# One transfer issued as two: the first weight load of a decode kernel in pieces of 16 and 112 partitions

## The chip, the cores and the metric

The kernel runs on one core of one Trainium2 chip. The metric is device time in microseconds (us): the median of three runs, 722.08 us before the change, the runs lying between 721.86 and 722.98 us. A core has five engines that this text names as the profile does: PE (TensorE, matrix products), DVE (VectorE), ACT (ScalarE), POOL (GpSimd) and SP (SyncE, which here only issues transfers). Sixteen DMA engines move data between the memory (HBM) and the on-chip tiles, which have 128 partitions.

## The reference

One decode step for two sequences, all in float32: attention over a cache of 4096 positions with 32 heads of 128, beside a small dense network, mixed by a gate.

```python
g = sigmoid((x * gate_w).sum(-1, keepdims=True))          # x: (2, 1, 576)
q = (x @ wq).reshape(B, 1, 32, 128).transpose(0, 2, 1, 3)   # wq: (576, 4096)
p = softmax(einsum("bhqd,bhkd->bhqk", q, k_cache) * 128 ** -0.5)
o = einsum("bhqk,bhkd->bhqd", p, v_cache)                    # caches: (2, 32, 4096, 128)
a = o.transpose(0, 2, 1, 3).reshape(B, 1, 4096) @ wo         # wo: (4096, 576)
b = gelu(x @ w1 + b1) @ w2 + b2                              # w1: (576, 4608)
return g * a + (1 - g) * b
```

The two caches are 134 MB each, the four weight matrices together some 40 MB. Every byte is used once.

## The kernel before, in words

**Ring.** One tile, `ring`, holds three slots of 128 partitions x 16384 floats (64 KB a partition, 8.4 MB a slot). Everything that comes from HBM in bulk lands there. The order of the transfers is written out by hand in `seq`: wq in two loads (`("wq", 0)` and `("wq", 1)`), w1 in three, then for each of sixteen units `i` a tile of the key cache and a tile of the value cache (`load_heads`, line 130), then three batches with w2 and wo (`load_last`, line 145). `load()` takes the next entry; every bulk transfer is issued by SP on one queue, in this order.

**The first transfer.** `load_w(wq, (4,), 0)` takes the first 512 rows of wq, four rows to a partition. Each partition gets 4 x 4096 floats in one piece, 65,536 bytes, and the transfer fills slot 0 as a whole: 128 partitions, 8.4 MB. It is the first instruction of SP's queue (line 119). The remaining 64 rows of wq follow as 128 partitions x 8 KB, then w1 as two loads of 128 x 36 KB and one of 128 x 9 KB, all from line 119.

**The small inputs.** ACT issues four kinds of small transfers on a queue of its own: `load_b1(0)` (line 195, four rows of 4.6 KB to partitions 0, 32, 64 and 96), two rows of x (line 200) and the gate weights (line 201). They are issued in the first microseconds, beside the first bulk transfer, and later `load_b1(1)` and b2 (line 294).

**Start of the computation.** PE turns x and the gate weights into columns (line 249), forms the gate sum (line 258), and then `proj` multiplies x with wq (line 282 into `qps`) as soon as all of the first load is there. From q, q's rows are spread over the partitions (`q_unit`), and `proj` does the same with w1 (line 282 into `hps`). Each of these steps frees a slot, and SP waits for that before it issues the next cache tile.

**Units.** For each unit DVE multiplies the key tile by q (`mul`, line 457), DVE and POOL reduce it (`red`, lines 461 to 463), DVE takes a maximum (`max_p`, line 467), ACT forms the exponentials (line 482), and PE multiplies them with the value tile (`av`, line 493). A new tile is issued when the one three places earlier in the ring has been used up (`load_next`).

**End.** The last three batches bring w2 and wo in ever smaller pieces; the last product is in line 415, the output leaves by line 438, two rows of 2.3 KB.

**Counters.** Each transfer counts its completion on one of eight counters for transfers issued by SP and ACT, taken in turn; a transfer that takes a counter again waits until the transfer that had it before has landed. Such waits stand on the issuing engine (SP or ACT), ahead of the transfer.

Of the kernel before, what the change touches and what calls it, by code (L numbers as in the profile page):

```python
# [12 lines left out]
P = 128  # L13
# [6 lines left out]
def kernel(  # L20
# [14 lines left out]
    nc = tc.nc  # L35
# [69 lines left out]
    used = {"w": 0, "t": (WQ + F) * D // P}  # L105
# [3 lines left out]
    def load_w(w, rows, c):  # L109
        if c < len(rows):  # L110
            n = rows[c] * w.shape[1]
            lo = sum(rows[:c]) * P
            src = w[lo:lo + rows[c] * P].rearrange("(p r) n -> p (r n)", r=rows[c])
        else:
            n = w.shape[1] // 2
            src = w[NX * P:].rearrange("q (e n) -> (q e) n", e=2)
        t = ring[:, used["w"]:used["w"] + n]
        used["w"] += n
        nc.sync.dma_start(t, src)
        return t  # L120

    def slot(n):
# [27 lines left out]
    def temp(n, parts=P):  # L150
        t = ring[:parts, used["t"]:used["t"] + n]
        used["t"] += n
        assert used["t"] <= SLOTS * SLOT
        return t
# [7 lines left out]
    def load():  # L162
        if not seq:
            return
        kind, i = seq.pop()
        if kind == "wq":
            wqt[i] = load_w(wq, ROWS[kind], i)
        elif kind == "w1":
            w1t[i] = load_w(w1, ROWS[kind], i)
        elif kind == "k":  # L170
            kt[i] = load_heads(k_cache, i)
        elif kind == "v":
            vt[i] = load_heads(v_cache, i)
        else:
            load_last(i)
        if kind in ("k", "v", "last"):
            held.append((kind, i))
# [41 lines left out]
    for j in range(NPB):  # L219
        t = cp.tile([P, NT * EB + 32 - EB], F32, name=f"p{j}")  # L220
# [156 lines left out]
    t = temp(NF * B).rearrange("p (r b) -> p r b", b=B)  # L377
# [223 lines left out]
```

## Time and profile before

| what | value |
|---|---|
| median of 3 runs | 722.08 us (721.86 to 722.98) |
| the profiled execution, first to last instruction (its span) | 720.1 us |
| mean granted TensorE clock in the span | 0.666 |
| bytes read from HBM | 308.59 MB, 429 GB/s over the span |
| busy share: PE, DVE, ACT, POOL | 33%, 72%, 5%, 20% |
| SP's queue of bulk transfers: share of the 16 DMA engines' time | 99.2% |

For the profiled execution only the span is given, and no device time of its own; the median of the unprofiled runs lies 2.0 us above the span. A group of lines in the profile reads: line, engine, operation, tile written <- tile read, count, busy time, mean duration, and the idle time ahead of it with what ended it. "SPq" and "ACTq" are the issuing sides of SP and ACT; a line with DMA_DIRECT2D is the issue of a transfer, not the transfer itself. The DMA lines give the mean busy share of the 16 DMA engines by slice of the window, in tenths.

### The profile page before, as it was taken

How to read it: one execution, taken by the hardware profiler on the slowest of the kernel's cores; microseconds unless marked ns; L12 is line 12 of the kernel's file. 1: busy time of each engine (PE TensorE's matmuls, PEld its weight loads, DVE VectorE, ACT ScalarE, POOL GpSimd, SP SyncE). 2: the span in 40 equal slices, each digit the busy share in tenths (PEclk: the TensorE clock that was granted, in tenths of full speed). 3: DMA queues.
4: the chain of work that ended last, by engine and by line, in shares of the span. 5: the costliest groups of instructions: out<-in, count | busy, mean ns of one | idle time of the engine just before them, and what ended most of it. 6: DMA issues, size and time to landing. Idle time of an engine off the chain costs nothing.

```text
span 720.1 us, 3893 instructions
## 1 busy us (share of the span) xinstructions
PE 237.1 (33%) x1661; PEld 72.7 (10%) x1661; DVE 517.7 (72%) x150; ACT 37.8 (5%) x141; POOL 143.2 (20%) x28
## 2 busy tenths in 40 slices
PE   0755022140516060604142140506060503324197
PEld 0321000010101010101010000101010101001033
DVE  0004969879696969696969879696969596978900
ACT  0010010100101010101010100101010101010000
POOL 1000130404050403022040404040503113040400
PEclk9967557575757575665757575757575665757589
DMA  9999999999999999999999999999999999999997
GB/s 409 411 443 430 433 440 415 459 416 451 422 444 420 437 433 426 442 430 440 434 433 440 426 434 433 430 433 434 440 430 444 423 448 422 444 426 430 422 427 299
DMA packets 7101, 308.84 MB, mean 429 GB/s; under 512 B 798, under 2 KB 1182, under 8 KB 1580
## 3 DMA queue, kind: packets, MB, share of 16 engines
q1 hardware_dynamic: 7060, 308.55, 99.2%
q8 instruction: 13, 0.21, 0.1%
q10 hardware_dynamic: 24, 0.05, 0.0%
q14 instruction: 4, 0.03, 0.0%
HBM read 308.59 MB, written 0.00 MB: 429 GB/s over the span
## 4 chain that ended last, share of the span: by engine, by line
DMA 46%; DVE 35%; PE 17%; ACT 1%; issue 1%; POOL 0%; ACTq 0%; DVEq 0%; SPq 0%; POOLq 0%
DMA ring<-in_A_k_cache_dram 39%; DVE ring L457 19%; DVE s L462 10%; PE av L493 9%; DVE s L463 5%; DMA ring<-in_A_wo_dram 3%; DMA ring<-in_gate_w_dram 3%; PE qps L282 2%; PE hps L282 2%; PE oall L511 1%; PE acc L346 1%; PE mt L472 1%; ACT p L482 1%; DMA ring<-in_B_b_dram 1%; PE qps L307 1%
## 5 line engine op out<-in xcount | busy, mean ns | idle before, releaser
L457 DVE TENSOR_TENSOR ring<-ring,q 128x16384 f32<-128x16384 f32 x16 | 275.6, 17225 | 102.2 <-DMA ring<-in_A_k_cache_dram 102.2
L461 POOL TENSOR_TENSOR ring<-ring 128x3968 f32<-128x3968 f32 x16 | 137.1, 8566 | 487.4 <-DVE ring L457 457.3
L462 DVE TENSOR_REDUCE s<-ring 128x66 f32<-128x8448 f32 x16 | 143.3, 8953 | 1.3
L493 PE MATMUL av<-ring,p 128*32 128x512 f32 x1024 | 134.4, 684 | 11.4 <-ACT p L482 6.1
L472 PE MATMUL mt<-idsc,m 128*128 128x128 f32 x32 | 12.7, 501 | 365.9 <-DVE m L467 365.9
L463 DVE TENSOR_REDUCE s<-ring 128x62 f32<-128x3968 f32 x16 | 68.4, 4276 | 0.0
L482 ACT ACTIVATE p<-s,bs 32x128 f32<-32x128 f32 x64 | 25.5, 398 | 483.0 <-DVE bs L476 481.8
L493 PEld LDWEIGHTS av<-ring,p 128*32 128x32 f32 x1024 | 35.8, 125 | 119.6 <-issue 102.9
L472 PEld LDWEIGHTS mt<-idsc,m 128*128 128x128 f32 x32 | 8.0, 312 | 382.1 <-DVE m L467 353.5
L330 PE MATMUL qb<-qm,spread 64*128 64x512 f32 x8 | 8.3, 1137 | 69.8 <-POOL qm L326 69.8
L511 PE MATMUL oall<-avs,pick 128*64 128x512 f32 x32 | 30.6, 1059 | 0.8 <-DVE avs L505 0.8
L505 DVE TENSOR_TENSOR avs<-av,selr 128x512 f32<-128x512 f32 x16 | 10.9, 681 | 15.9 <-PE av L493 15.9
L369 DVE TENSOR_TENSOR ring<-hps,ring 128x384 f32<-128x384 f32 x3 | 1.7, 559 | 17.4 <-PE hps L282 17.3
L240 DVE COPY ring<-ring 3x64 f32<-3x64 f32 x2 | 0.3, 182 | 19.0 <-DMA ring<-in_gate_w_dram 19.0
L326 POOL TENSOR_TENSOR qm<-qall,mine 64x512 f32<-64x512 f32 x4 | 4.1, 1034 | 46.2 <-ACT qall L309 46.2
L301 DVE COPY ring<-ident 128x8 f32<-128x8 f32 x8 | 0.7, 169 | 16.9 <-DMA ring<-in_B_b_dram 16.9
L482 ACT ACTIVATION_READ_ACCUMULATOR p<-s,bs 32x1 f32 x64 | 11.8, 184 | 0.0
L282 PE MATMUL qps<-ring 128*32 128x512 f32 x80 | 11.6, 746 | 0.0
L282 PE MATMUL hps<-ring 128*32 128x384 f32 x120 | 11.5, 547 | 0.0
L346 PE MATMUL acc<-ring,hg 128*2 128x288 f32 x144 | 11.4, 453 | 0.0
L437 DVE COPY ring<-res 2x144 f32<-2x144 f32 x2 | 0.6, 300 | 12.7 <-PE res L415 12.7
L330 PEld LDWEIGHTS qb<-qm,spread 64*128 64x128 f32 x8 | 2.0, 307 | 72.9 <-POOL qm L326 72.9
(80 smaller groups left out, 75.2 us busy)
## 6 DMA issues: line engine op xcount, KB each, us to landing
ring<-in_B_w_dram SPq DMA_DIRECT2D x2, 4608.0 KB, 34.5
ring<-in_B_w_dram SPq DMA_DIRECT2D x2, 4032.0 KB
ring<-in_A_wo_dram SPq DMA_DIRECT2D x2, 2880.0 KB, 19.3
ring<-in_B_w_dram SPq DMA_DIRECT2D x1, 2304.0 KB, 13.3
ring<-in_A_wo_dram SPq DMA_DIRECT2D x2, 864.0 KB
ring<-in_B_w_dram SPq DMA_DIRECT2D x1, 1152.0 KB
ring<-in_A_wo_dram SPq DMA_DIRECT2D x1, 1152.0 KB
ring<-in_A_wq_dram SPq DMA_DIRECT2D x1, 1024.0 KB, 24.1
```

What stands on the lines that cost most here:

```text
L282: nc.tensor.matmul(ps[32 * j:32 * j + 32, :width], lhs, ts[c][:, o:o + width], start=(k == 0), stop=last, skip_group_check=True,)
L330: nc.tensor.matmul(ps, spread, t.rearrange("p u d -> p (u d)"), start=True, stop=True)
L346: nc.tensor.matmul(acc[o:o + m], lhsT, rhs[:, s * DS:(s + 1) * DS], start=start, stop=stop, skip_group_check=True)
L457: nc.vector.tensor_mul(kt[i], kt[i], qs[i].unsqueeze(1).to_broadcast([P, R, DH]))
L461: nc.gpsimd.tensor_add(t[:, :, :DH2], t[:, :, :DH2], t[:, :, DH2:])
L462: nc.vector.tensor_reduce(st[i][:, HALVED:], kt[i][:, HALVED:], AX.X, ALU.add)
L463: nc.vector.tensor_reduce(st[i][:, :HALVED], t[:, :, :DH2], AX.X, ALU.add)
L472: nc.tensor.matmul(mt[i], mx[i].to_broadcast([P, P]), idsc, start=True, stop=True)
L482: nc.scalar.activation(p[w, :, e * RB:(e + 1) * RB], st[i][w].rearrange("p (t c) -> p t c", c=RB), AF.Exp, bias=bias[i][w, e:e + 1], scale ...
L493: nc.tensor.matmul(ps[32 * j:32 * j + 32], p[:, EB * t:EB * t + 32], vt[i][:, RB * t:RB * (t + 1)].rearrange("p r d -> p (r d)"), start=(t ...
L505: nc.vector.tensor_mul(t, avs[i].rearrange("p (r d) -> p r d", d=DH), selr.unsqueeze(2).to_broadcast([P, RB, DH]))
L511: nc.tensor.matmul(oall, pick[:, NO - E - i * E:2 * NO - E - i * E], avs[i].rearrange("p r d -> p (r d)"), start=(i == 0), stop=(i == N - ...
```

## The change

In `load_w`, the transfer that fills the start of the ring is issued as two: partitions 0 to 15 (1.05 MB) first, then partitions 16 to 127 (7.34 MB). All other loads have `first = P` and are issued as before. The destination, the data and everything that reads them stay. SP's queue has one more transfer, and the transfers behind it take the next of the eight counters, so some of the waits on counters that SP and ACT make name another earlier transfer.

```diff
             src = w[NX * P:].rearrange("q (e n) -> (q e) n", e=2)
         t = ring[:, used["w"]:used["w"] + n]
+        first = 16 if used["w"] == 0 else P
         used["w"] += n
-        nc.sync.dma_start(t, src)
+        for a, z in ((0, first), (first, P)):
+            if a < z:
+                nc.sync.dma_start(t[a:z], src[a:z])
         return t
```

## The prediction

> **What bounds the kernel now.** I began with the page: the span, its slices, the queues.
>
> ```profile
> span 720.1 us, 3893 instructions
> PE 237.1 (33%) x1661; PEld 72.7 (10%) x1661; DVE 517.7 (72%) x150; ACT 37.8 (5%) x141; POOL 143.2 (20%) x28
> DMA  9999999999999999999999999999999999999997
> q1 hardware_dynamic: 7060, 308.55, 99.2%
> HBM read 308.59 MB, written 0.00 MB: 429 GB/s over the span
> ```
>
> The reader is to see that no engine comes near the span (DVE has 72%), while SP's queue q1 has the DMA engines at work in 99.2% of it. The busy time by stages says how fast they then go; the columns are the stretch, its length, busy time by engine, TensorE clock, DMA share, GB/s.
>
> ```profile
> 22.00:40.00 18.00, 15.10 (x100) 6.24 (x100) 1.36 (x8) 1.35 (x3) 0.00 (x0) 1.00 1.04 448
> 70.00:680.00 610.00, 172.03 (x1024) 46.82 (x1024) 501.11 (x92) 31.20 (x123) 140.03 (x19) 0.63 1.00 434
> ```
>
> In 610 us the share is 1.00 at 434 GB/s: 27.1 GB/s on each of 16 engines, so a row of 65,536 bytes takes 2.42 us, and a tile of 128 rows, eight to an engine, 19.3 us. 308.55 MB at that rate are 711 us. Of the span of 720.1 us 9 are left: the time before the first byte, the part after the last, and what single engines fall behind. Nothing in the middle can catch up, since there is no idle time to take back. So whatever the stream loses at the start stands at the end, in full; and the first transfer is where the change is.
>
> The start of the stream comes from the queues' view of the first 2.2 us (40 slices of 0.055 us) and from SP's issues.
>
> ```profile
> DMA  0000000000000000000000000000000999990090
> DMA packets 14, 0.92 MB, mean 417 GB/s; under 512 B 0, under 2 KB 0, under 8 KB 0
> ...
> 0.74 0.86 SPq L119 DMA_DIRECT2D ring<-in_A_wq_dram  x2
> 1.65 13.97 SPq L119 DMA_DIRECT2D ring<-in_B_w_dram  x3
> 36.78 0.33 SPq L130 DMA_DIRECT2D ring<-in_A_k_cache_dram  x1
> 62.06 0.33 SPq L130 DMA_DIRECT2D ring<-in_A_v_cache_dram  x1
> ```
>
> The first issue begins at 0.74 us; the first packets start in the 32nd slice, at 1.71 to 1.76, and by 2.2 us 14 of the first 16 have. So the head is 1.0 us for the first engine and 1.5 for the last.
>
> **The change part by part.** *The first bytes come earlier.* What a transfer of few rows needs from issue to first packet shows at the end, where the output's two rows go to an idle queue (issue from the timeline, then the slices of 717 to 721 us, 0.1 us each).
>
> ```profile
> 718.02 0.33 SPq L438 DMA_DIRECT2D out_dram<-ring  x1
> ...
> GB/s 0 0 0 0 0 0 0 0 0 0 0 0 0 0 0 0 0 23 23 0 0 0 0 0 0 0 0 0 0 0 0 0 0 0 0 0 0 0 0 0
> ```
>
> Packets at 718.7 to 718.9 after an issue at 718.02: 0.7 to 0.8 us. A transfer of 16 rows lies between two and 128, much nearer to two. The first engine gains 0 to 0.3 us, the last up to 0.5 if its first row no longer comes behind those of the others. I take 0.3.
>
> *One more issue on SP.* Two issues of line 119 take 389 and 415 ns:
>
> ```profile
> L119 SPq DMA_DIRECT2D ring<-in_A_wq_dram x2: 389/402/415, 0.7 to 1.2; - x2
> ```
>
> The second piece is thus issued at about 1.18 us, ready at about 2.2 (its head of 1.0), and each engine has its first row of 2.42 us until past 4: no gap. What is queued behind it on SP moves by 0.4 us: the rest of wq and w1, first needed when 19.3 us of wq have passed. Cost: nothing; without that cover it would be 0.4 us.
>
> *Waits on counters.* With one more transfer the counters shift by one place: w1's second and third load no longer wait for the first b1 and then the first row of x, but for the first and then the second row of x.
>
> ```profile
> SPq L119 <- DMA ring<-in_B_b_dram: 8.4, 1, 8.4
> SPq L119 <- DMA ring<-in_A_x_dram: 4.4, 1, 4.4
> 3.54 19.32 DMA ring<-in_gate_w_dram
> L119 SPq DMA_DIRECT2D ring<-in_B_w_dram x3: 328/328/424, 1.6 to 15.3; - x3
> DMA to landing us min/median/max: 24.1/29.3/34.5
> ```
>
> The second row of x lies ahead of the gate's on ACT's queue, which landed at 22.9 us. SP is then held until 23 at the latest instead of 15.3, and behind it stand w1's last load and the first key tile (issued at 36.8 anyway). The engines have wq and w1's first load until about 36 (issued at 1.65, landed after 34.5). Cost: nothing. On ACT, `load_b1(1)` and b2 now wait for the first piece and the first b1, long landed at 38.5 us when they are issued.
>
> *Sixteen rows at once into sixteen neighbouring partitions.* This is the part that decides. Before, the 16 engines always work on a tile of 128 partitions. The first piece puts one row on each engine, and all 16 write into one eighth of the tile. No transfer in this trace does that in bulk, so the cost is bounded. From below: if the 27.1 GB/s are the engine's own, where it writes is of no matter, the piece takes 2.42 us, and costs 0. From above: if they are the width of a way into the tile that eight partitions share (128 partitions, 16 such ways), sixteen partitions have two ways, eight rows go through each, and the piece takes 19.3 us: 16.9 too many, while the other ways lie idle. That w1's rows of 36 KB go at the rate of the caches' rows of 64 KB (448 GB/s at a share of 1.04 in 22 to 40 us, so 431, and 434 after) speaks for a fixed width, but it can't say on which side it stands. Between two ways and one for each row I take the middle, 10.9 us for the piece, so 8.5 too many.
>
> [...]
>
> *112 rows behind them.* Seven rows on each engine, 16.9 us if each has its way to itself: with the first piece's 2.42 the same total as before. But 112 rows cut into sixteen sevens no longer agree with groups of eight, so engines will at times meet on one way. Each round in which they do costs one row more, 2.42 us; between none and all seven rounds, 0 to 16.9 us. A seven lies mostly within one group of eight, so I take one round, 2.4.
>
> *The sum.* 8.5 + 2.4 − 0.3 = 10.6 us. The span goes from 720.1 to 730.7; the median is 2.0 above the span (722.08), so 732.7.
>
> *Whether the rest passes it on.* The computation shifts as a whole, since the gate's row and the first load land later alike. The tight place is the value tile's issue at 62.06, which waits for PE's work on w1. The tile in front of it is used from 70.44:
>
> ```profile
> 70.44 17.22 DVE L457 TENSOR_TENSOR ring<-ring,q 128x16384 f32<-128x16384 f32 x1 [0.61 <-DMA ring<-in_A_k_cache_dram]
> ...
> 695.00 20.69 DMA ring<-in_A_wo_dram
> 715.74 1.97 PE res L415 x40
> 717.72 0.28 ACT ring L437
> ```
>
> The issue has 8.4 us in hand, and both ends shift together. At the end the chain of waits hangs on the last wo piece, then 2.3 us of PE and ACT: the loss arrives there undiminished.
>
> **The rivals.** *The way into the tile is no limit (not slower).* For it: a fixed 27.1 GB/s per engine is just what an engine's own limit looks like, and DVE, POOL and PE work on the tile at the same time without denting the 1.00. Then the first and the second piece cost nothing, the head gains 0 to 0.5 us: 721.6 to 722.1, say 721.8. It decides at the point where the first piece lands: before 6 us it is this one. Against it: 16 writers in an eighth of the tile is untested here, and the equal rate also fits the tile's side.
>
> *The second piece is the dear one.* If its rows are dealt in turn, row 0 to engine 0, row 1 to engine 1, every round is again 16 neighbouring partitions and costs what the first piece does: eight rounds of 8.5 too many, 68 us, 790. If only some rounds collide it lies between 742 and that. For it: only the name of the transfer is in the profile, not how its rows are dealt. Against it: a deal like that would make the plain tile of 128 rows slow as well, and it goes at 434 GB/s.
>
> *The split falls on fewer engines.* If an engine kept its habit of eight rows, the first piece would be on two engines and the second on fourteen. Were the two among the fourteen, they would carry sixteen rows: 16.9 us more, 739. This is the same upper bound by another way, and I count it with the main case. [...]
>
> *A real gain.* The whole head is 1.0 us to 1.5; a gain of more than 1.4 us would need nearly all of it.
>
> **How the numbers follow.** Writers crowd in sixteen partitions, 724 to 742: 0.62. No limit there, 721.4 to 722.6: 0.27. Second piece dear, above 742: 0.08. Real gain: 0.03. The balance for the first is that the change takes the stream from the only shape in which the trace shows full rate, and that any shared way costs whole microseconds; the middle of its bounds gives 732.7, and its own range is 1.9 to 19.3 us over 722.08 (a lost row of 2.4 less half a microsecond; 16.9 + 2.4), 724 to 741.4. To hold 8 in 10 the range must take in the case without a limit: 721.4 to 742. About 0.2% (1.4 us) can be told from no change in this kernel. Faster by more: 0.03; within: 0.27; slower: 0.70.
>
> **What would show it.** In the profile after: the first piece should land near 12 us instead of 4 to 5, and the first 20 us should show less than the 434 GB/s, by about 3.7 MB in all (8.5 us); if those slices are full, my step is wrong and the time is the old one. The gate's row should land at about 30 instead of 22.9, `qps` begin after 34, and every later line, the key tiles' too, stand about 10 us later, with the DMA share still 1.00 in the 610 us of the middle. If the lines shift by over 20 us, the second piece is to blame; if the first piece lands early and the rest late, likewise. A gap in the stream between 22 and 70 us would show that the waits or the issue at 62 us cost what I put at nothing.

## The result, and the profile after

The changed kernel takes 742.12 us (median of 4 runs, 741.81 to 743.58) against 721.99 us before (4 runs): a ratio of 1.0282, 95% interval 1.0269 to 1.0294, or 20.1 us more. The profiled execution is the longest of the four, 743.58 us; its span is 741.8 us, 21.7 more than that of before, so the views below show some 1.5 us more than the medians do.

The page of the kernel after:

```profile
span 741.8 us, 3898 instructions
...
DMA  9989999999999999999999999999999999999996
GB/s 171 269 349 455 414 435 449 417 435 443 424 435 442 432 424 445 438 422 438 436 431 435 435 432 435 431 438 431 436 438 428 435 436 435 431 435 440 415 425 262
...
q1 hardware_dynamic: 7076, 308.55, 98.9%
...
HBM read 308.59 MB, written 0.00 MB: 416 GB/s over the span
```

Against the page of before, the row of busy DMA engines has hardly changed (99.2% became 98.9%). The loss shows in the bytes alone: the first three slices of 18.5 us move 171, 269 and 349 GB/s, and from the fourth on everything is as before. The stages say it with times (stretch, length, busy time by engine, TensorE clock, DMA share, GB/s). The first 40 us of the stream before:

```profile
2.00:42.00 40.00, 15.10 (x100) 6.24 (x100) 2.95 (x15) 2.63 (x4) 0.76 (x2) 1.00 0.96 411
```

The same stretch and the long middle after:

```profile
2.00:42.00 40.00, 0.00 (x0) 0.00 (x0) 1.59 (x7) 1.28 (x1) 0.76 (x2) 1.00 0.93 207
92.00:700.00 608.00, 172.86 (x1024) 46.82 (x1024) 499.18 (x92) 31.21 (x123) 140.01 (x19) 0.62 1.00 434
```

40 us at 207 instead of 411 GB/s are 8.2 MB too little, 18.8 us of stream at 434; the first 2 us, at 197 instead of 393, add 0.9 us. The 608 us of the middle are at full rate. The share is 0.93 at 207 GB/s and 0.96 at 411: a DMA engine that waits with a row in hand counts as busy here, so the share can't show such a loss.

The first 12 us, in 40 slices of 0.3 us, show single rows. A row's bytes are put down where it starts; 218 GB/s in a slice is one row. Every burst is a round in which the 16 engines start one row each (the second burst of before, 1092, 2185 and 218, is 16 rows). First before, then after:

```profile
GB/s 874 0 0 0 0 0 0 0 0 1092 2185 218 0 0 0 0 0 889 2231 437 0 0 0 0 0 874 1748 874 0 0 0 0 0 655 1974 874 0 0 0 0
DMA packets 77, 4.48 MB, mean 373 GB/s; under 512 B 4, under 2 KB 4, under 8 KB 9
```

```profile
GB/s 218 1748 218 0 0 0 0 0 0 0 0 0 0 0 0 0 0 0 0 0 0 0 0 218 0 218 218 655 218 874 874 218 0 0 0 0 0 0 0 0
DMA packets 42, 1.70 MB, mean 142 GB/s; under 512 B 16, under 2 KB 16, under 8 KB 16
```

Before, the bursts stand 2.4 us apart (4.7, 7.1, 9.5, 11.9 us). After, the first burst is followed by the second at 8.9 to 11.6 us only: the first piece held every engine for 7 to 9 us, where before it was about 3.

```profile
0.74 1.31 SPq L122 DMA_DIRECT2D ring<-in_A_wq_dram  x3
2.09 35.80 SPq L122 DMA_DIRECT2D ring<-in_B_w_dram  x3
54.82 0.33 SPq L133 DMA_DIRECT2D ring<-in_A_k_cache_dram  x1
81.73 0.33 SPq L133 DMA_DIRECT2D ring<-in_A_v_cache_dram  x1
...
3.51 38.75 DMA ring<-in_gate_w_dram
...
46.31 8.49 PE qps L285 x64
...
54.82 37.21 DMA ring<-in_A_k_cache_dram
...
716.64 20.67 DMA ring<-in_A_wo_dram
...
739.30 0.27 ACT ring L440
```

These are SP's issues and three places of the chain of waits. The gate's row lands at 42.3 us instead of 22.9, PE begins on wq at 46.3 instead of 26.9, the first key tile and the first value tile are issued at 54.8 and 81.7 instead of 36.8 and 62.1, and the key tile is there at 92.03 (70.4 before). The last wo transfer is as long as it was (20.67 us, 20.69 before).

### The profile page after: what moved, and what is told of

Read it like the earlier page. It is cut to its first block, busy times and chain, and to the rows that moved or that the text cites. A ratio compares the mean times of both kernels' runs of the same rounds, so it can differ in the third digit from the quotient of the medians.

```text
span 741.8 us, 3898 instructions
## 1 busy us (share of the span) xinstructions
PE 236.1 (32%) x1661; PEld 72.4 (10%) x1661; DVE 517.8 (70%) x150; ACT 37.9 (5%) x141; POOL 143.2 (19%) x28
## 3 DMA queue, kind: packets, MB, share of 16 engines
q1 hardware_dynamic: 7076, 308.55, 98.9%
## 4 chain that ended last, share of the span: by engine, by line
DMA 50%; DVE 33%; PE 14%; ACT 1%; issue 1%; POOL 0%; ACTq 0%; DVEq 0%; POOLq 0%
DMA ring<-in_A_k_cache_dram 37%; DVE ring L460 19%; PE av L496 10%; DVE s L465 10%; DMA ring<-in_gate_w_dram 5%; DMA ring<-in_B_w_dram 5%; DVE s L466 5%; DMA ring<-in_A_wo_dram 3%; PE qps L285 1%; ACT p L485 1%; PE oall L514 1%; PE mt L475 1%; PE acc L349 0%; DVE m L470 0%; PE zps L261 0%
## 5 line engine op out<-in xcount | busy, mean ns | idle before, releaser
L508 DVE TENSOR_TENSOR avs<-av,selr 128x512 f32<-128x512 f32 x16 | 10.9, 681 | 15.6 <-PE av L496 15.6
L285 PE MATMUL hps<-ring 128*32 128x384 f32 x120 | 11.9, 562 | 0.0
L349 PE MATMUL acc<-ring,hg 128*2 128x288 f32 x144 | 10.6, 422 | 0.4 <-DMA ring<-in_B_w_dram 0.4
## 6 DMA issues: line engine op xcount, KB each, us to landing
ring<-in_B_w_dram SPq DMA_DIRECT2D x2, 4608.0 KB, 55.6
```

The costliest lines, as they stand in the source:

```text
L285: nc.tensor.matmul(ps[32 * j:32 * j + 32, :width], lhs, ts[c][:, o:o + width], start=(k == 0), stop=last, skip_group_check=True,)
L349: nc.tensor.matmul(acc[o:o + m], lhsT, rhs[:, s * DS:(s + 1) * DS], start=start, stop=stop, skip_group_check=True)
L508: nc.vector.tensor_mul(t, avs[i].rearrange("p (r d) -> p r d", d=DH), selr.unsqueeze(2).to_broadcast([P, RB, DH]))
```

## The experiments

Three theories. **A**: the 16 engines share ways into the tile by partition, and a piece of few partitions puts several on one way (an assumption: no run shows a way itself). **B**: the memory side, the order in which the engines read. **C**: any second transfer in the place of one. All kernels change only how the first load is issued, in `load_w`; the other loads are as in the kernel before (the `if` and `else` lines that see to this are not shown, and the labels in comments are this text's). e1 was timed in eleven runs, the others in one each. The kernel before lay between 721.67 and 722.98 us in all its runs, so a difference of 1 us between single runs says nothing.

**e1, cut by columns.**

```diff
-        nc.sync.dma_start(t, src)
+        for a, z in ((0, 2048), (2048, n)):
+            nc.sync.dma_start(t[:, a:z], src[:, a:z])
```

> The first load is cut by columns, not by partitions: 128 partitions x 8 KB first, then 128 x 56 KB. Theory A (writers that meet on a shared way into the tile): each engine keeps its rows, so nothing is lost: 722 us, within 1. Theory B (the memory side: engines that read rows in another order than the plain one hinder each other): the rows stay with their engines here too, 722 to 724. Theory C (any second transfer in the place of one costs, by its counters and its issue): about 742, as in the changed kernel.

722.0 us against 721.85, ratio 1.0002, interval 0.9993 to 1.0011. Theory C is out: a second transfer with its issue, its counter and the shifted waits costs nothing that can be measured, as long as every engine keeps its rows. Nor does a small first piece gain anything.

**e2, halves; e3 and e4, eight pieces.**

```diff
+        for a, z in ((0, 64), (64, P)):                                   # e2
+            nc.sync.dma_start(t[a:z], src[a:z])
+        for j in range(8):                                               # e3
+            nc.sync.dma_start(t[16 * j:16 * j + 16], src[16 * j:16 * j + 16])
+        for j in range(8):                                               # e4
+            nc.sync.dma_start(t[j::8], src[j::8])
```

> The first load as partitions 0 to 63, then 64 to 127: four rows for each engine and piece. A: half of the tile has half of the ways, two writers on each, so a row takes 4.8 us instead of 2.4 in both pieces: 8 x 2.4 = 19 us more, 741, less if the engines drift so that both halves are in work at once. B: less than in the changed kernel, 722 to 735, as rows are in larger groups. C: 742.

> The first load as eight pieces of 16 neighbouring partitions, each read from 16 neighbouring rows. A: every piece costs what the first piece of the changed kernel did, 8 to 9.7 us against 2.4: 45 to 58 us more, 767 to 780. B: the same. C: seven extra transfers, 722 + 7 x 20 = 860 if each costs what one did, or 742 if only being split counts.

> Eight pieces of 16 rows again, but piece j takes partitions j, j+8, ... j+120 (and the same rows of the source). A: the sixteen writers stand on half of the ways or on all: 722 to 741, in any case well under the eight neighbouring pieces. B: depends on the read order alone, rows are 512 KB apart instead of 64 KB: below the eight neighbouring pieces if neighbours in memory are the trouble. C: as the eight neighbouring pieces.

Measured: 744.52, 777.0 and 743.44 us; before, beside them, 721.85. e3 lies where A put it; e2 and e4 came 2 to 4 us above what A gave (741, and 722 to 741). The same slices of 2 to 14 us, for e2, e3, e4 in this order:

```profile
GB/s 2403 437 655 0 0 0 0 0 0 0 0 0 0 0 0 437 1092 1092 874 0 0 0 0 0 0 0 0 0 0 0 0 0 234 874 1123 671 655 0 0 0
```

```profile
GB/s 0 1529 0 0 0 0 0 0 0 0 0 0 0 0 0 0 0 0 0 0 0 0 0 0 218 218 218 655 437 1092 655 0 0 0 0 0 0 0 0 0
```

```profile
GB/s 1529 655 655 655 0 0 0 0 0 0 0 0 0 0 0 218 437 1092 1529 218 0 0 0 0 0 0 0 0 0 0 0 0 218 234 265 2185 655 0 0 0
```

Halves and spread pieces have a round about every 5 us (6.5 to 7.4, 11.6 to 12.8), the neighbouring pieces one in 9. In all three a load is eight rounds of one row on each engine, so the totals give the price of a round beyond its 2.42 us: (744.52 − 721.85) / 8 = 2.8 us for e2, 2.7 for e4, 6.9 for e3. That is near one and three rows of 2.42 us more, 2.4 and 7.3 us, as if two and four writers took turns: an estimate from these totals.

**e5 and e6, tile and source apart.**

```diff
+        for j in range(8):                                               # e5
+            nc.sync.dma_start(t[j::8], src[16 * j:16 * j + 16])
+        for j in range(8):                                               # e6
+            nc.sync.dma_start(t[16 * j:16 * j + 16], src[j::8])
```

> Eight pieces of 16 rows as before, but piece j reads 16 neighbouring rows of wq (16j to 16j+15) and writes them to partitions j, j+8, ... (the rows of wq so reach other partitions than x expects). Theory A (tile side): as the run with eight spread pieces, 743.4, since the writers stand as there. Theory B (memory side): as the run with eight neighbouring pieces, 777, since the reads are those.

> The counterpart: piece j reads rows j, j+8, ... of wq and writes 16 neighbouring partitions (rows again in other places than x expects). A: 777, as the eight neighbouring pieces. B: 743.4, as the eight spread ones.

743.15 and 776.8 us. In both, rows of wq land in other partitions than x expects, so q is not the right one; the transfers and the work are the same in size. Each time goes with its partitions (743.44 and 777.0), to 0.3 us, and not with its reads. Theory B is out; what counts is the partitions that are written.

**e7, e8, e12: three pieces, the first with 64 rows at three offsets.**

```diff
+            nc.sync.dma_start(t[32:96], src[32:96])        # e7; e8: 36:100; e12: 40:104
+            nc.sync.dma_start(t[0:32], src[0:32])          #     e8:  0:36;  e12:  0:40
+            nc.sync.dma_start(t[96:128], src[96:128])      #     e8: 100:128; e12: 104:128
```

> Three pieces: partitions 32 to 95, then 0 to 31, then 96 to 127. [...] If any piece of 64 rows goes at half speed, about 742.

> [...] The total, with odd pieces behind, 735 to 760.

> [...]

Totals 732.82, 750.48 and 758.88 us. (e12 was put on record after e9 to e11, which follow.) The issue and landing of e7's first and third piece, then of e12's first:

```profile
L120 SPq DMA_DIRECT2D ring<-in_A_wq_dram x1: 635/635/635, 0.7 to 0.7; - x1
...
DMA to landing us min/median/max: 13.6/13.6/13.6
```

```profile
L122 SPq DMA_DIRECT2D ring<-in_A_wq_dram x1: 412/412/412, 2.0 to 2.0; - x1
...
DMA to landing us min/median/max: 32.4/32.4/32.4
```

```profile
L120 SPq DMA_DIRECT2D ring<-in_A_wq_dram x1: 641/641/641, 0.7 to 0.7; - x1
...
DMA to landing us min/median/max: 23.7/23.7/23.7
```

e7 is 9 us under the 742 at which a piece of 64 rows at half speed would have put it. Its first piece keeps the full rate: the 64 rows, four to an engine, land 13.6 us after their issue (at 14.3 us), and the two pieces of 32 take until 34.4 us, 20.1 us for four rounds, 5.0 us each. So the loss depends on which 64 partitions are written, not on their number alone: those from 32 on have what those from 0 or 64 on lack (e2). Nor are the rows dealt to the engines in turn: rounds of 16 neighbours, at the 9.3 us a row of e3, would have made four rounds 37 us. How the rows are dealt, and which partitions hinder each other, no run shows; no row names the engine of a transfer. Slices of 2 to 14 us for e8, then e12:

```profile
GB/s 2185 1092 218 0 0 0 0 0 0 0 1748 1311 0 0 0 0 437 0 1575 1545 0 0 0 0 0 0 218 2403 437 0 0 0 0 437 218 2220 218 246 0 0
DMA packets 101, 4.95 MB, mean 413 GB/s; under 512 B 19, under 2 KB 19, under 8 KB 24
```

```profile
GB/s 1748 1092 655 0 0 0 0 0 0 0 0 0 0 0 0 655 1311 1092 437 0 0 0 0 0 0 0 0 0 0 0 0 0 0 717 1748 655 437 0 0 0
DMA packets 52, 3.16 MB, mean 264 GB/s; under 512 B 0, under 2 KB 0, under 8 KB 4
```

In e8 14 of the 16 rows of a round start together every 2.4 to 2.7 us (5.0, 7.4, 10.1), and 4.95 MB are started; two rows are late, at 6.8 us, and two more at 11.9. In e12 no row starts between 2.9 and 6.5 or between 7.7 and 11.9 us, and 3.16 MB are started, as few as in e2. The landing alone doesn't tell the two apart: 23.1 us after the issue in e8, 23.7 in e12. So the first piece moved by four partitions held up two rows of a round, and moved by eight all 16, in one run each. Why four partitions more make this difference the runs don't show.

**e9, e10, e11: 112, 96 and 48 rows first.**

```diff
+            nc.sync.dma_start(t[16:128], src[16:128])      # e9
+            nc.sync.dma_start(t[0:16], src[0:16])
+            nc.sync.dma_start(t[0:96], src[0:96])          # e10
+            nc.sync.dma_start(t[96:128], src[96:128])
+            nc.sync.dma_start(t[32:80], src[32:80])        # e11
+            nc.sync.dma_start(t[0:32], src[0:32])
+            nc.sync.dma_start(t[80:128], src[80:128])
```

> The same two pieces, the 112 partitions (16 to 127) first, the 16 (0 to 15) behind them: shows what the 112 rows cost with nothing ahead of them. [...] If all 16 engines are slowed together, as the changed kernel's late landing suggests: all land at 31 to 34 us and the total stays at 742 to 744.

> Partitions 0 to 95 first (six rows for each engine), then 96 to 127. [...] The 32 rows behind take two rounds at half speed, 4.8 us more than without. [...]

> Partitions 32 to 79 first (three rows each), then 0 to 31, then 80 to 127. [...]

743.06, 742.59 and 753.04 us; before, beside them, 722.83 in a single run, 1 us above the medians of 721.83 to 722.1 beside the other kernels. Slices of 2 to 14 us for e9 and e10:

```profile
GB/s 874 218 0 0 0 218 0 0 0 0 0 0 0 218 1092 218 1529 218 0 218 0 0 0 0 0 0 0 0 0 218 686 874 1123 437 0 0 218 0 0 0
DMA packets 42, 2.51 MB, mean 209 GB/s; under 512 B 0, under 2 KB 0, under 8 KB 4
```

```profile
GB/s 218 437 0 0 0 0 0 0 0 0 0 0 0 218 1311 1092 437 218 218 0 0 0 0 0 0 0 0 0 0 0 15 905 1108 874 437 218 0 0 0 0
DMA packets 39, 2.31 MB, mean 193 GB/s; under 512 B 0, under 2 KB 0, under 8 KB 4
```

In e10 the bursts stand some 5 us apart (2.0, 6.2 to 6.5, 11.3 to 11.6) with next to nothing between: all 16 engines are slowed together. e9 shows the 112 rows at the same pace from the start, and costs what the change costs, as put down for 16 engines slowed together (742 to 744). e11's first piece, three rows to an engine:

```profile
L120 SPq DMA_DIRECT2D ring<-in_A_wq_dram x1: 392/392/392, 0.7 to 0.7; - x1
...
DMA to landing us min/median/max: 18.3/18.3/18.3
```

It landed 18.3 us after its issue at 0.7, far above three rows at 2.42 us, 7.3. The total is 30.2 us more than before; the last piece, the 48 rows from partition 80 on, is the dearest (it landed at 52.9 us, the piece ahead of it at 29.2).

The change costs 20.1 us, and e9 20.2 (743.06 − 722.83; 21.2 against 721.85). With 6.9 for the piece of 16, by e3, some 13 us are left to the 112 rows. e10 costs 19.8 (20.7 against 721.85) for eight rounds, 2.5 to 2.6 us a round.

The rounds of the 112 rows can be read one by one. The slices of 2 to 42 us, 1 us each, for e9, whose 112 rows come first, then for the change (a row of 64 KB is 66 GB/s here):

```profile
GB/s 328 66 0 0 721 328 0 0 66 805 197 0 459 524 66 459 264 328 0 131 524 328 66 0 262 461 328 0 66 459 264 197 66 0 0 0 16 41 74 98
```

```profile
GB/s 655 0 0 0 0 0 0 197 524 328 0 0 0 210 857 0 0 0 262 786 0 723 197 131 0 786 131 131 0 393 527 131 0 197 590 131 131 0 57 215
```

In e9 the 16 rows of the first round start at 2.1 us on average, and, worked out from these slices, those of the next six at 6.8, 11.6, 15.1, 18.4, 22.8 and 27.6; the rows of the small piece follow at 32.3. So the seven rounds last 4.7, 4.8, 3.5, 3.3, 4.4, 4.8 and 4.7 us: the two short ones are the third and the fourth. In the change (10.6, 16.3, 21.3, 23.9, 27.9, 32.3, 36.7, good to some 0.3 us) the same two are the shortest, 2.6 and 4.0 against 4.4 to 5.7. The seven rounds of e9 last 30.2 us instead of 16.9, 13.3 more. Why the third and the fourth lose least, no run shows.

## Why the prediction was right or wrong

The direction and the place held: slower, by which partitions of the tile are written at once (e5, e6), with the loss at the start and carried whole to the end. The size didn't: 732.7 was forecast with a range to 742.0, and 742.12 was measured. That the top of the range is so near is chance: it took the 16 rows at their bound (16.9; they cost 6.9) and the 112 rows at one round (2.4; they cost 13). With both bounds it would have been some 756.

- *The term that failed: "112 rows behind them", 2.4 us.* It cost about 13 (20.1 − 6.9 = 13.2; 13.3 by e9's rounds). The step that failed is the number of rounds in which engines meet: one of seven, because a seven lies mostly within one group of eight. That doesn't follow even on the prediction's own map: 112 partitions are fourteen groups of eight, so 16 engines at work must meet in every round, which at its own price is its upper bound, 16.9. In e9 all seven rounds take longer than 2.4 us, the first two and the last three by 2.0 to 2.4 us, the third and the fourth by about 1. The price of a round, 2.42 us, was near. That map failed too: on it the pieces of e4, with rows eight partitions apart, would have a way for each row, and they cost 2.7 us a round. But the term didn't fail by that. That the whole stream pays for such a round had been put in without a reason; in e12 all 16 rows of a round come late together, in e8 two.
- *Sixteen rows, 8.5 us too many.* Between its bounds and near: 6.9 by e3, a row of 9.3 us instead of 10.9. The sign named for this piece held: its engines were to be free near 12 us, and they start their next rows between 8.9 and 11.6.
- *"Writers crowd", 0.62, against "no limit", 0.27.* Decided by e5 and e6. The rival "second piece dear" was right about where two thirds of the time went, and its sign (lines that shift by over 20 us) came true; it was wrong about why: a deal in turn would have given 68 us, and the 112 rows lost some 13; e7's first piece landed in 13.6 us where a deal in turn would have needed 37. "Fewer engines" is out: all 16 rows of the first piece start between 1.7 and 2.9 us, and an engine takes 2.4 us or more for one.
- *The head, −0.3.* No gain. The first 2.2 us of the kernel after:

```profile
DMA  0000000000000000000000000000000099000000
...
DMA packets 6, 0.39 MB, mean 179 GB/s; under 512 B 0, under 2 KB 0, under 8 KB 0
```

The first packets start in the 33rd slice, one later than before, and six have by 2.2 us where it was 14. The output's two rows at the end were not a measure for this place.

- *One more issue.* Right: three issues of wq take 1.31 us where two took 0.86, no gap follows, and e1 shows the whole of it at 0.

```profile
L122 SPq DMA_DIRECT2D ring<-in_A_wq_dram x3: 379/399/430, 0.7 to 1.6; - x3
L122 SPq DMA_DIRECT2D ring<-in_B_w_dram x3: 328/328/767, 2.1 to 37.6; - x3
...
SPq L122 <- DMA ring<-in_A_x_dram: 34.3, 2, 25.6
```

- *Waits on counters.* They moved as forecast, from b1 to the rows of x; but "23 at the latest" became 37.6, since x landed later too (that it shares the slowed engines is likely, but argued). The cover grew with it: w1's first load, issued at 2.1, landed 55.6 us later. Cost nothing, as put down.
- *Whether the rest passes it on.* Right. The first key tile is used from 92.05 instead of 70.44, 21.6 us later, the span ends 21.7 later, and the middle runs at 434 GB/s. In the lines that I named as tests, the gate's row was to land near 30 and `qps` to begin after 34; 42.3 and 46.3 told at once that the first load had lost nearly twice the 10.6 us that I gave it.

## What to carry to other kernels

Cut a bulk load along the free dimension, not along partitions: 128 partitions in each piece cost nothing (e1, 722.0 us against 721.85), while pieces of 16, 96 or 112 partitions, and of 64 from partition 0, 64 or 40 on (e2, e12), ran at a quarter to little more than half of the rate (a row of 2.42 us took 9.3 us in pieces of 16 neighbours, about 5 in those of 64 and 96, 4.3 on average in those of 112). The 64 from partition 32 on kept it (e7, landed in 13.6 us), and those from 36 on did for all but two rows of a round (e8). In a kernel whose stream never rests, such a loss at the start is paid in full at the end (20.1 us here). And where the busy share of the DMA engines stays at 99%, look at GB/s by slice: that row of the page showed where the 20 us went, and the busy share didn't.

## What the hardware showed that I had not expected

- A first piece of 64 rows from partition 40 on slowed all 16 engines to about 5 us a row (e12); the one from 36 on held up two rows of a round (e8), and the one from 32 on none (e7).
- A small first transfer did not start sooner: with 16 rows the first packets come at 1.76 us instead of 1.71, and e1's first piece of 8 KB rows brought no gain either.
- The issues of e2, with 64 rows each, took longer than those of 128, 112 or 16 rows:

```profile
L121 SPq DMA_DIRECT2D ring<-in_A_wq_dram x2: 568/572/575, 0.7 to 1.4; - x2
```

568 and 575 ns, against 379 to 430 for the three issues of wq in the changed kernel. The number of rows alone isn't the reason: 32 rows took 571 in e7 but 406 in e11. The cause stays open. The engines had work in all of them, so it cost nothing.
